# Query copies one unit sooner, and another order of eight small matmuls in odd units

## The chip, the cores and the metric

The kernel runs on one core of a Trainium2 chip. The metric is the device time of one execution in microseconds (us). One execution of the kernel before was also recorded by the hardware profiler, and the profile and the trace below are of that one.

## The reference

Two attention blocks are computed on inputs of 2048 tokens and 448 features, forward and backward, from bfloat16 data. Block A is linear attention with 16 heads. Block B is softmax attention with 16 query heads of 28 features that share one key head and one value head:

```
q = heads(x @ wq);  k = x @ wk;  v = x @ wv
p = softmax(q k^T * 28**-0.5);  o = p v;  out = concat_heads(o) @ wo
```

The outputs are the forward result of both blocks (side by side) and the gradients for all eight inputs, given the gradient of the result. The two changes lie in block B, in the stage that computes the scores, the softmax and their gradients.

## The kernel before

Block A and the projections of block B come first. Then comes the stage of interest, which we call the core. It is one loop over u, written out by hand in the order in which each engine is to take its instructions (a manual schedule: nothing is reordered by a planner). The queries are cut into 64 blocks b of 256 tokens and two heads (b = 8 * qc + pair, where qc counts the eight slices of 256 tokens and pair the eight pairs of heads). Each block is walked in 8 units of 256 keys, so there are 512 units, and u % 8 is the unit's place in its block. A unit u works on several things that are at different stages:

- **Scores.** rows_SD (lines 683 to 705) issues eight small matmuls. Four are score quarters S: head 0 and head 1, each for two groups of 128 keys, of 32 x 128 weights and 256 columns. We write S0a, S0b for head 0 and S1a, S1b for head 1. ScalarE turns them into exponentials: exp0 (line 955) takes both S0 quarters, exp1 (line 997) both S1 quarters. In the trace these are the tiles aacc (scores) and eT (exponentials).
- **Gradients of the probabilities.** The other four matmuls of rows_SD are gradient quarters D0a, D0b, D1a, D1b for the unit w = u - 16. In the trace they are agen<-doT. VectorE multiplies D0 with the exponentials (line 967, into dsT). D1 is first copied by ScalarE (line 971, tile cp) and then multiplied by GpSimd (line 972). A pair of banks holds D, one for each head, so D0 of a unit waits until line 967 of the unit before has read its bank, and D1 until line 971 of the unit before has.
- **Transposes and sums.** VectorE transposes dsT of unit u - 18 (line 1041, into dsx). In odd units dk_m sums the key gradient on TensorE (sixteen matmuls agen<-dsx,qX); in even units o_dq sums the output and the query gradient (sixteen matmuls from eT and dsT).
- **Once per block.** At u % 8 = 1 VectorE copies the block's output sums (line 983); at u % 8 = 2 TensorE transposes them into a spare score bank (line 809) and VectorE copies them out of it (line 817), and GpSimd does three small products (lines 821, 830, 831). The next unit's S0a goes into that same bank. At u % 8 = 4 GpSimd does two more small products (lines 836, 837), and at u % 8 = 6 TensorE transposes their result don (line 845) and VectorE copies it (line 852).
- **Query copies.** dk_m takes its weights from a tile qX, one for each slice of 256 tokens, in which the queries are transposed. It is made one slice ahead, in four groups g. For each group GpSimd makes two copies with gaps into a staging tile qst (line 856, called at line 979), in two units one after the other, and SyncE then issues a DMA transpose from qst to qX (line 860, called at line 1002). There is one tile qst for all groups, so the first copy of a group waits until the transfer of the group before has landed. This runs in the units with u % 64 from 30 to 55, for u below 448: two units out of every eight.
- **Transposes of the exponentials.** At every u % 4 = 3 SyncE issues a DMA transpose of four units' exponentials (line 999, eN<-eT), ahead of line 1002 in the same unit. TensorE reads it at least nine units later. The transposes of lines 860 and 999 go through SyncE's one queue in the order in which they are issued.

In rows_SD, d[0] picks S (0) or D (1) and d[1] the head; a pair's first occurrence in the list is its quarter a, its second is b. S uses two of TensorE's four groups of 32 rows, D the other two, and each head one of them: so S0, S1, D0 and D1 have a group of rows each.

Of the kernel before, what the change touches and what calls it, by code (L numbers as in the profile page):

```python
# [25 lines left out]
def kernel(  # L26
# [624 lines left out]
    with ExitStack() as cs_:  # L651
# [23 lines left out]
        def mmt(out, lhsT, rhs, pos, start, stop):  # L675
            nc.tensor.matmul(out, lhsT=lhsT, rhs=rhs, start=start, stop=stop, tile_position=pos,  # L676
                             skip_group_check=True)

        def blk(b):
            qc, pair = divmod(b, 8)  # L680
            return qc, pair, pair // 2, pair % 2

        def rows_SD(u, sp, dp):
            b, tp = divmod(u, 8)
            w = u - 16
            qc, pair, g, hp = blk(b)
            todo = [(0, 0), (0, 1)] * 2 + [(1, 0), (1, 1)] * 2
            if u % 2 == 0:
                todo = [(0, 0), (0, 1), (1, 0)] * 2 + [(1, 1)] * 2
            seen = {}  # L690
            for d in todo:
                if (dp if d[0] else sp) is None:
                    continue
                k, h = d
                t2 = seen.get(d, 0)
                seen[d] = 1
                t = 2 * tp + t2
                tc_ = slice(t * P, (t + 1) * P)
                oc = slice(t2 * 256, (t2 + 1) * 256)
                r = 64 * (1 - hp if k else hp) + 32 * h  # L700
                if k:
                    mmt(dp[h][:, oc], vT_rep[r:r + 32, tc_], doT[w // 8][r:r + 32, :], (r, 0), True, True)
                else:
                    mmt(sp[h][:, oc], kT_rep[r:r + 32, tc_], qT_B[g][r:r + 32, qc * 256:(qc + 1) * 256],
                        (r, 0), True, True)
# [216 lines left out]
        with tc.manual_schedule():  # L922
# [8 lines left out]
            for u in range(NU + 28):  # L931
# [4 lines left out]
                dp = DB if hasD else None  # L936
                spare = SB[(2 * u + 2) % 3] if hasS else DB[u // 4 % 2] if u > 530 else SB[2]
                rows_SD(u, sp, dp)
                if u % 2 == 0:
                    b, n = divmod(u - 20, 8)  # L940
# [22 lines left out]
                if hasD:  # L963
# [6 lines left out]
                    cp = pc_.tile([P, 512], BF16, name="cp")  # L970
                    nc.scalar.activation(out=cp[:, :], in_=dp[1][:, :], func=ACT.Copy)  # L971
                    nc.gpsimd.tensor_tensor(out=dst[:, 1, :], in0=cp[:, :], in1=ew[:, 1, :], op=ALU.mult)  # L972
                gq, iq = divmod(u % 64 - 30, 8)
                qq = u // 64 + 1
                if 0 <= gq < 4 and u < 448:
                    if gq == 0 and iq == 0:
# [183 lines left out]
```

## Time and profile before

| | us |
|---|---|
| median of 3 runs (lowest to highest) | 1047.6 (1046.28 to 1047.8) |
| the profiled execution | 1045.81 |
| its span, from the first instruction to the end of the last | 1044.1 |

| engine | busy us | share of the span |
|---|---|---|
| TensorE (PE) | 1003.6 | 96% |
| VectorE (DVE) | 887.4 | 85% |
| ScalarE (ACT) | 865.8 | 83% |
| GpSimd (POOL) | 811.9 | 78% |

The core's units run from about 207 us to about 997 us of the span. A row of the timeline gives the start in us, the duration in us, the engine, the line, the operation, the tile it writes and those it reads, how many instructions of that kind are merged into the row, and in brackets the idle time of the engine just before and what ended it. Records of one engine can overlap by a little, since the next instruction starts while the last one drains. SPq is SyncE's queue. The profiler models the ends of matmuls, so for TensorE only the starts are read here.

### The profile page before, as it was taken

How to read it: one execution, taken by the hardware profiler on the slowest of the kernel's cores; microseconds unless marked ns; L12 is line 12 of the kernel's file. 1: busy time of each engine (PE TensorE's matmuls, PEld its weight loads, DVE VectorE, ACT ScalarE, POOL GpSimd, SP SyncE). 2: the span in 40 equal slices, each digit the busy share in tenths (PEclk: the TensorE clock that was granted, in tenths of full speed). 3: DMA queues.
4: the chain of work that ended last, by engine and by line, in shares of the span. 5: the costliest groups of instructions: out<-in, count | busy, mean ns of one | idle time of the engine just before them, and what ended most of it. 6: DMA issues, size and time to landing. Idle time of an engine off the chain costs nothing.

```text
span 1044.1 us, 40103 instructions
## 1 busy us (share of the span) xinstructions
PE 1003.6 (96%) x16236; PEld 485.1 (46%) x16245; DVE 887.4 (85%) x1780; ACT 865.8 (83%) x1743; POOL 811.9 (78%) x1106
## 2 busy tenths in 40 slices
PE   9999999998899999999999999999999999999998
PEld 5555555434444444444444444444444444444444
DVE  7898500669899999999999999999999999999942
ACT  6463132599999999999999999999999999999632
POOL 8601282238898999999999989999998999888860
PEclk9999999999999999999999999999999999999999
DMA  9879999199999999999999999999999999999983
GB/s 266 150 134 195 184 232 213 32 161 205 189 183 198 191 188 195 198 190 189 201 198 197 190 190 203 194 193 198 202 184 201 191 199 192 192 194 197 218 159 90
DMA packets 689059, 195.15 MB, mean 187 GB/s; under 512 B 670409, under 2 KB 686689, under 8 KB 688873
## 3 DMA queue, kind: packets, MB, share of 16 engines
q1 hardware_dynamic: 680392, 179.97, 103.7%
q0 software_dynamic: 4544, 9.46, 3.1%
q10 hardware_dynamic: 3936, 3.16, 1.1%
q8 instruction: 127, 2.08, 0.8%
q14 instruction: 60, 0.48, 0.2%
HBM read 12.60 MB, written 10.84 MB: 22 GB/s over the span
## 4 chain that ended last, share of the span: by engine, by line
PE 37%; DVE 28%; POOL 17%; issue 9%; ACT 8%; DMA 0%; DVEq 0%; POOLq 0%; ACTq 0%
PE agen L81 13%; POOL dsT L972 12%; DVE dsT L967 12%; DVE dsx L1041 10%; PE agen L676 8%; PE aacc L676 7%; PE aacc L81 6%; ACT cp L971 4%; ACT eT L997 2%; DVE doT L852 1%; DVE R L986 1%; POOL qst L856 1%; POOL prod L821 1%; PE aacc L809 1%; DVE Dq L835 1%
## 5 line engine op out<-in xcount | busy, mean ns | idle before, releaser
L972 POOL TENSOR_TENSOR dsT<-cp,eT 128x512 bf16<-128x512 bf16 x512 | 584.1, 1156 | 45.5 <-ACT cp L971 39.8
L1041 DVE STREAM_TRANSPOSE dsx<-dsT 128x512 f32<-128x512 f32 x512 | 357.2, 698 | 8.7 <-POOL dsT L972 5.9
L676 PEld LDWEIGHTS <-R 32*128 32x128 bf16 (+1 forms) x9104 | 245.1, 94 | 246.5 <-issue 195.4
L967 DVE TENSOR_TENSOR dsT<-agen,eT 128x512 bf16<-128x512 f32 x512 | 340.3, 665 | 9.7 <-PE agen L676 4.1
L971 ACT ACTIVATE cp<-agen 128x512 bf16<-128x512 f32 x512 | 326.2, 637 | 12.2 <-PE agen L676 10.3
L955 ACT ACTIVATE eT<-aacc 128x512 bf16<-128x512 f32 x512 | 325.3, 635 | 12.6 <-PE agen L676 6.7
L997 ACT ACTIVATE eT<-aacc 128x512 bf16<-128x512 f32 x512 | 332.4, 649 | 0.0
L676 PE MATMUL agen<-dsx,qX 32*32 32x512 bf16 x4024 | 264.0, 376 | 0.0
L676 PE MATMUL agen<-doT,R 32*128 32x256 bf16 x2048 | 241.6, 269 | 4.1 <-DVE dsT L967 2.6
L676 PE MATMUL aacc<-R,R 32*128 32x256 bf16 (+1 forms) x2240 | 208.3, 267 | 18.9 <-DVE doT L852 7.5
L676 PE MATMUL agen<-dsT,R 128*32 128x256 bf16 x2048 | 155.8, 273 | 0.3 <-POOL dsT L972 0.2
L676 PE MATMUL agen<-eT,R 128*32 128x256 bf16 x2048 | 155.7, 273 | 0.1
L676 PEld LDWEIGHTS <-qX 32*32 32x32 bf16 x4096 | 78.2, 89 | 112.4 <-issue 54.1
L676 PE MATMUL aacc<-eN,don 128*32 128x512 bf16 x1024 | 90.6, 387 | 0.0
L81 PEld LDWEIGHTS <-R 128*128 128x128 bf16 x517 | 40.9, 98 | 41.4 <-issue 11.0
L856 POOL COPY qst<-R 128x512 bf16<-128x512 bf16 x56 | 34.3, 613 | 11.2 <-DMA qX<-qst 5.7
L81 PE MATMUL agen<-R,R 128*128 128x448 bf16 (+1 forms) x174 | 41.1, 360 | 1.7 <-issue 0.6
L676 PEld LDWEIGHTS <-don 128*32 128x32 bf16 x1024 | 20.9, 93 | 40.6 <-issue 40.6
L821 POOL TENSOR_TENSOR prod<-R,oTs 128x128 f32<-128x128 bf16 x64 | 27.5, 430 | 9.0 <-DVE oTs L817 9.0
L586 DVE TENSOR_TENSOR osb<-R 32x512 bf16<-32x512 bf16 x4 | 1.7, 414 | 35.4 <-ACT R L583 35.4
L262 POOL TENSOR_SCALAR wdq<-wdq 128x448 bf16<-128x448 bf16 x16 | 21.1, 1327 | 12.8 <-DVE phiT L243 12.8
L427 POOL COPY pk<-R 128x256 bf16<-128x256 bf16 x4 | 1.6, 400 | 37.7 <-DVE R L389 37.7
(235 smaller groups left out, 1001.2 us busy)
## 6 DMA issues: line engine op xcount, KB each, us to landing
eN<-eT SPq DMA_TRANSPOSE x128
xa<-in_A_x_dram SPq DMA_DIRECT2D x8, 224.0 KB
ga<-in_grad_out_dram SPq DMA_DIRECT2D x4, 448.0 KB
out_dram<-osb ACTq DMA_DIRECT2D x16, 112.0 KB
xa<-in_grad_out_dram POOLq DMA_DIRECT2D x4, 448.0 KB, 8.3
out_dram<-wdq POOLq DMA_DIRECT2D x8, 224.0 KB, 5.1
eT<-in_grad_out_dram SPq DMA_DIRECT2D x4, 448.0 KB
eT<-in_B_x_dram SPq DMA_DIRECT2D x4, 448.0 KB
```

Of the source, the lines that this page charges most:

```text
L81: nc.tensor.matmul(out_ap, lhsT=lhsT, rhs=rhs, start=start, stop=stop, tile_position=(0, 0))
L262: nc.gpsimd.tensor_scalar(out=wq_n[:, st, 0:D], in0=wq_n[:, st, 0:D], scalar1=1.0, scalar2=None, op0=ALU.min)
L676: nc.tensor.matmul(out, lhsT=lhsT, rhs=rhs, start=start, stop=stop, tile_position=pos, skip_group_check=True)
L809: nc.tensor.transpose(onp[:, qb, :, :].rearrange("p h c -> p (h c)"), oTs[0:64, qb * P:(qb + 1) * P], identF[0:64, 0:64], tile_position=(0 ...
L821: nc.gpsimd.tensor_tensor(out=prod[b][:], in0=dnv, in1=os_, op=ALU.mult)
L856: eng.tensor_copy(out=st.rearrange("p (b s) a j -> p b s a j", s=2)[:, :, s, :, :], in_=src.unsqueeze(2).to_broadcast([P, 4, 4, 32]))
L955: nc.scalar.activation(out=eT(u)[:, 0, :], in_=sp[0][:, :], func=ACT.Exp, scale=scale)
L967: nc.vector.tensor_tensor(out=dst[:, 0, :], in0=dp[0][:, :], in1=ew[:, 0, :], op=ALU.mult)
L971: nc.scalar.activation(out=cp[:, :], in_=dp[1][:, :], func=ACT.Copy)
L972: nc.gpsimd.tensor_tensor(out=dst[:, 1, :], in0=cp[:, :], in1=ew[:, 1, :], op=ALU.mult)
L997: nc.scalar.activation(out=eT(u)[:, 1, :], in_=sp[1][:, :], func=ACT.Exp, scale=scale)
L1041: nc.vector.transpose(out=dsx[b][:, tp, :, :, :].rearrange("p h t c -> p (h t c)").bitcast(F32), in_=dsT[y][:, :, :].rearrange("p h c -> p ...
```

## The change

Two lines are edited, and no work is added or removed.

In odd units the eight matmuls of rows_SD are issued in the order S0a S1a S0b D1a S1b D1b D0a D0b; before, it was S0a S1a S0b S1b D0a D1a D0b D1b. Even units keep S0a S1a D0a S0b S1b D0b D1a D1b.

The query copies run in the units with u % 64 = 29 and 30, 37 and 38, 45 and 46, 53 and 54, one unit sooner than before, and the DMA transpose of a group is issued in the second of them. That unit has u % 4 = 2, so the transpose of a group now goes into SyncE's queue one unit ahead of a transpose of exponentials; before, it went in right behind that one. The allocation of the tile qX moves with it.

```
@@ rows_SD
-            todo = [(0, 0), (0, 1)] * 2 + [(1, 0), (1, 1)] * 2
+            todo = [(0, 0), (0, 1), (0, 0), (1, 1), (0, 1), (1, 1), (1, 0), (1, 0)]
             if u % 2 == 0:
                 todo = [(0, 0), (0, 1), (1, 0)] * 2 + [(1, 1)] * 2
...
@@ the loop over u
-                gq, iq = divmod(u % 64 - 30, 8)
+                gq, iq = divmod(u % 64 - 29, 8)
                 qq = u // 64 + 1
                 if 0 <= gq < 4 and u < 448:
                     if gq == 0 and iq == 0:
                         qX[qq] = (pqb_ if qq % 2 else pqa_).tile([P, 4, 2, 512], BF16, name="qX")
                     if iq < 2:
                         qc_copy(nc.gpsimd, qst, qq, gq, iq)
...
                     if 0 <= gq < 4 and iq == 1 and u < 448:
                         qc_T(qst, qq, gq)
```

More of the change, by code (lines that the diff above doesn't have):

```diff
@@ L686, in rows_SD @@
             qc, pair, g, hp = blk(b)
-            todo = [(0, 0), (0, 1)] * 2 + [(1, 0), (1, 1)] * 2
+            todo = [(0, 0), (0, 1), (0, 0), (1, 1), (0, 1), (1, 1), (1, 0), (1, 0)]
             if u % 2 == 0:
@@ L972 @@
                     nc.gpsimd.tensor_tensor(out=dst[:, 1, :], in0=cp[:, :], in1=ew[:, 1, :], op=ALU.mult)
-                gq, iq = divmod(u % 64 - 30, 8)
+                gq, iq = divmod(u % 64 - 29, 8)
                 qq = u // 64 + 1
```

## The prediction

> **What bounds the kernel now.** I read the page first, for who is busy and who waits, then the core in strips of equal work, then single units in the timeline.
>
> ```profile
> L955 ACT ACTIVATE eT<-aacc 128x512 bf16<-128x512 f32 x512 | 325.3, 635 | 12.6 <-PE agen L676 6.7
> ...
> L856 POOL COPY qst<-R 128x512 bf16<-128x512 bf16 x56 | 34.3, 613 | 11.2 <-DMA qX<-qst 5.7
> ```
>
> ScalarE's exp0 (L955) was kept waiting by TensorE for up to 12.6 us in all. It is the first of ScalarE's three instructions in a unit, so a wait there holds up the unit. GpSimd idled 11.2 us ahead of its 56 query copies (L856). The next view shows that the two go together. I cut the core at the starts of exp0 into strips of 32 units, and took those seven in which query copies run (units 32 to 63 of each 64); ScalarE's exp0 alone is counted, so that each strip holds 32 of them.
>
> ```profile
> core 0: us, ACT busy (x), PEclk, DMA share, GB/s
> 252.83:303.36 50.53, 19.78 (x32) 1.00 1.14 186
> ...
> 541.36:588.48 47.12, 20.80 (x32) 1.00 1.18 198
> ...
> 732.64:779.76 47.12, 20.80 (x32) 1.00 1.19 187
> ...
> sum 339.34, ACT 142.32; mean ACT 20.33
> ```
>
> The same work takes 47.12 us in two strips, up to 50.53 in others, and 339.34 in the seven. If all took 47.12, it would be 329.84: so 9.5 us are lost in strips with query copies, though two strips with as many copies lose nothing against the best. What differs is a wait, and the view of the copies' line names it.
>
> ```profile
>   DMA qX<-qst: 5.7, 7
>   DVE dsx L1041: 3.4, 2
>   DVE dsT L967: 2.1, 1
> ```
>
> Ten first copies of a group waited, 5.7 + 3.4 + 2.1 = 11.2 us. Seven are put down to the transfer from qst. Of the other three VectorE is named; a copy needs nothing of VectorE there, so I read the same transfer into them. SyncE's queue shows how the transfers stand, and the timeline of one group how its lateness ends at ScalarE.
>
> ```profile
> 645.81 11.16 SPq L999 DMA_TRANSPOSE eN<-eT  x2
> 657.03 1.30 SPq L860 DMA_TRANSPOSE qX<-qst  x1
> 658.43 11.01 SPq L999 DMA_TRANSPOSE eN<-eT  x2
> 669.54 1.26 SPq L860 DMA_TRANSPOSE qX<-qst  x1
> ```
>
> ```profile
> 656.85 0.71 DVE L1041 STREAM_TRANSPOSE dsx<-dsT 128x512 f32<-128x512 f32 x1 [0.47 <-POOL dsT L972]
> ...
> 657.32 0.23 PE L845 MATMUL aacc<-identB,don 128*32 128x128 bf16 x2 [0.16 <-POOL don L837]
> ...
> 658.51 0.28 PE L676 MATMUL aacc<-R,R 32*128 32x256 bf16 x2 [0.47 <-DVE doT L852]
> ...
> 658.92 0.60 ACT L955 ACTIVATE eT<-aacc 128x512 bf16<-128x512 f32 x1 [0.57 <-PE agen L676]
> ...
> 660.99 0.61 POOL L856 COPY qst<-R 128x512 bf16<-128x512 bf16 x1 [0.41 <-DMA qX<-qst]
> ...
> 674.02 0.61 POOL L856 COPY qst<-R 128x512 bf16<-128x512 bf16 x1 [1.29 <-DVE dsx L1041]
> ```
>
> SyncE works without a pause: two transposes of exponentials (11.16 and 11.01 us), then one for the queries. The query transfer issued at 657.03 releases the copy at 660.99, and that of 669.54 the copy at 674.02: 4.0 and 4.5 us from issue to use. While GpSimd is behind, VectorE waits for its product (0.47), TensorE for the small product don and for VectorE's copy of it (0.16 and 0.47), and ScalarE in the end for scores (0.57 us idle).
>
> In undisturbed units all three of ScalarE, VectorE and TensorE are nearly full: 47.12 / 32 = 1.47 us a unit. One unit with u % 8 = 1, which is odd (the second of the strip that begins at 541.36), shows the chain:
>
> ```profile
> 541.49 1.16 POOL L972 TENSOR_TENSOR dsT<-cp,eT 128x512 bf16<-128x512 bf16 x1
> ...
> 541.84 0.63 ACT L971 ACTIVATE cp<-agen 128x512 bf16<-128x512 f32 x1
> ...
> 542.27 0.70 DVE L1041 STREAM_TRANSPOSE dsx<-dsT 128x512 f32<-128x512 f32 x1
> ...
> 542.41 0.28 PE L676 MATMUL aacc<-R,R 32*128 32x256 bf16 x2
> 542.42 0.28 PE L676 MATMUL agen<-doT,R 32*128 32x256 bf16 x1
> 542.51 0.27 PE L676 MATMUL aacc<-R,R 32*128 32x256 bf16 x1
> 542.53 0.26 PE L676 MATMUL agen<-doT,R 32*128 32x256 bf16 x1
> ...
> 542.54 0.36 PE L676 MATMUL agen<-doT,R 32*128 32x256 bf16 x2
> ...
> 542.82 0.64 ACT L955 ACTIVATE eT<-aacc 128x512 bf16<-128x512 f32 x1
> ...
> 542.89 0.68 DVE L967 TENSOR_TENSOR dsT<-agen,eT 128x512 bf16<-128x512 f32 x1
> ...
> 543.49 0.41 DVE L983 COPY oTs<-agen 64x256 f32<-64x256 f32 x1
> ...
> 543.81 0.28 PE L676 MATMUL aacc<-R,R 32*128 32x256 bf16 x2
> ...
> 543.82 0.69 DVE L1041 STREAM_TRANSPOSE dsx<-dsT 128x512 f32<-128x512 f32 x1
> ...
> 544.26 0.66 ACT L955 ACTIVATE eT<-aacc 128x512 bf16<-128x512 f32 x1
> 544.44 0.64 DVE L967 TENSOR_TENSOR dsT<-agen,eT 128x512 bf16<-128x512 f32 x1
> ...
> 545.02 0.27 DVE L817 COPY oTs<-aacc 128x128 f32<-128x128 f32 x1
> ...
> 545.34 0.28 PE L676 MATMUL aacc<-R,R 32*128 32x256 bf16 x2
> ...
> 545.75 0.65 ACT L955 ACTIVATE eT<-aacc 128x512 bf16<-128x512 f32 x1
> ```
>
> At 542.41 S0a and S1a start, at 542.42 D0a. Then D1a waits until ScalarE's copy of the unit before is done (541.84 + 0.63 = 542.47) and starts at 542.53, D0b at 542.54, D1b 0.1 later. VectorE's product of D0 starts at 542.89, in VectorE's own turn: its six instructions from 542.27 to 545.02 start as fast as each lets the next. The last (L817) frees the bank for the S0a of 545.34, and exp0 follows at 545.75. So whatever makes the product of 542.89 late makes exp0 of two units on late.
>
> **The order of matmuls.** D1a is now ahead of S1b, D1b and both quarters of D0, and all of these are queued behind its wait. S0 keeps its place, so exp0 has its scores as before. S1b now follows D1a (542.53), and exp1 takes it only after exp0 and cp: no cost. D1 cannot be sooner, since its wait ends when it ended; its cover is ScalarE's own turn. D0 is what moves: D0a no longer starts at 542.42, ahead of the wait, but behind it at about 542.54, and D0b, in the same rows, one matmul (0.11) later, at 542.65 in place of 542.54. What this costs needs the time from D0b to VectorE's start where VectorE really waits for it; the unit 40 units later shows that:
>
> ```profile
> 601.74 0.37 PE L676 MATMUL agen<-doT,R 32*128 32x256 bf16 x3
> ...
> 602.06 0.69 DVE L967 TENSOR_TENSOR dsT<-agen,eT 128x512 bf16<-128x512 f32 x1 [0.20 <-PE agen L676]
> ```
>
> D0b at 601.74 (the row's second, right behind D1a), product at 602.06 after 0.20 us idle: 0.32 us. So in the unit above the product could start at 542.65 + 0.32 = 542.97 instead of 542.89: 0.08 later. VectorE runs without a gap from there to L817, S0a waits for L817, and exp0 for S0a; so 0.08 us a block. In a unit like the one 40 later, where VectorE already waits, it is 0.11. In the other odd units VectorE is itself late (at u % 8 = 5 D0a waits for it, and then the order does not matter) or has been shifted by the same 0.08 already. From the 64 blocks I take off two that have no gradients yet and, as an estimate from the code, some twelve in which a wide output projection brings the scores after ScalarE's copy, so that D1a does not wait: 50 x 0.08 = 4.0 us. The bounds are 0, if the trace's idle-free VectorE hides it, and 50 x 0.11 = 5.5. The eight odd units of the drain, without scores, are not on this chain; at 0.11 each they would add 0.9.
>
> That sum lets matmuls pass each other: D0a, fifth in the old order, started at 542.42, ahead of S0b at 542.51, which was issued before it but waited for S0a's rows. If they kept the order of issue, the new list would take one step more (rivals, below). The Trainium skill says just that: "TensorE: Matmul & The Clock Gate", section "Part 3: Packing small matmuls — row/col tiling", has matmuls start and end in program order, with only weight loads pulled ahead. The rows here disagree in the starts, and the measurement decides; the ends are modelled and show nothing.
>
> **The copies.** No copy is saved: 56 at 613 ns before and after. What moves is the transfer: it is issued one unit (1.47 us) sooner and ahead of one transpose of exponentials, half of 11.16 = 5.6 us, instead of behind it. The next group's copy asks 1.47 sooner, too. So the transfer gains about 5.6 us on its reader, if the copy is done by the time SyncE comes to it; even if SyncE has to wait a unit for the copies, 4 us are left. The ten waits have a mean of 1.1 us, and none is above 3.4 (two make up that sum). I count them as gone, and with them the 9.5 us; for a remainder in the first strip, where SyncE is furthest behind, I take off 0.5: gain 9.0. The other bound is 0.
>
> What is late next? On GpSimd each copy is moved past one product (L972), so two products a group end 0.6 us later than before. The one that starts at 541.49 ends at 542.65, and VectorE transposes its result at 543.82: 1.2 us of cover for 0.6. On SyncE one transpose in two goes 1.3 us later (the 1.27 and 1.30 above); its reader comes nine units later or more, over 13 us. If SyncE waits for a copy, only such transposes stand behind it. The tile qX is taken a unit sooner, at u % 64 = 29, where its last reader was at 25. All this I cost at nothing.
>
> **The sum.** -9.0 + 4.0 = -5.0 us. The profiled execution, 1045.81, would be 1040.8. The median of the runs is 1.8 us above it, and I put the change on the median: 1047.6 - 5.0 = 1042.6.
>
> **The rivals.**
>
> *The order costs nothing.* VectorE's product has other slack, or D0a still slips ahead of the wait. Then 1047.6 - 9.5 = 1038.1. For it: 0.08 us is small. Against it: idle-free rows up to L817. Chance 0.13.
>
> *The order takes most of the gain.* If VectorE is pushed by the whole step of 0.11 in every block, or by part of it in two places of a block without catching up in between, that is 64 x 0.11 = 7.0, and 1047.6 - 9.0 + 7.0 = 1045.6. VectorE has little slack anywhere, which speaks for it; in the unit shown 0.03 of the 0.11 is slack, which speaks against. Chance 0.15.
>
> *Matmuls keep the order of issue (slower).* Then in odd units S0a, then S0b D1a S1b, then D1b D0a, then D0b take a step of 0.11 more than before, on TensorE itself. It has almost no room: exp0 started 542.82 - 542.41 = 0.41 after S0a and again 545.75 - 545.34 = 0.41 where TensorE set it, and 544.26 - 543.81 = 0.45 behind an odd unit, so 0.04 is free. It decides from 0.04 on: 0.07 x 4 odd units x 60 blocks = 17 us, and 1047.6 - 9.0 + 17 = 1055.6. This is the page's rule named above. The starts speak against it: chance 0.10.
>
> *The copies fall at a worse place (slower).* At u % 8 = 5 GpSimd is still behind from the three small products and don. If the products of units 5 and 6 then come after VectorE asks for them, each group costs what is over the cover, and the gain is turned into a new wait. It decides when GpSimd is 0.6 us further behind than in the unit above; at 0.3 us of new wait for each of the 28 groups, 8.4 in all, it comes to 1047.6 - 9.0 + 8.4 + 4.0 = 1051.0. The two strips without waits, where GpSimd does the same work, speak against it. Chance 0.09.
>
> *The waits do not go.* The transfer lands late whatever its place. Then 1047.6 + 4.0 = 1051.6; the steady 4.0 to 4.5 us from issue to use speak against it. Chance 0.03.
>
> **How the numbers follow.** The forecast has 0.50, at 1040 to 1044.6. Something within 0.2% (2.1 us, about what a measurement of this kernel can tell from no change) comes mostly from the second rival. Faster by more: 0.50 + 0.13 + half of the second, 0.70. Same: 0.09. Slower: the last three, 0.22 less what stays near nothing, 0.21. The range runs from the first rival, 1038.0, to 1050.5, so that only the in-order case and most of the last two lie above it.
>
> **What would show it.** Right: no idle time before L856 from the transfer; strips of 32 units with copies as long as those without; at u % 8 = 1 D0b about 0.12 us behind D1a, VectorE idle for some 0.08 before L967, and exp0 at u % 8 = 3 that much later; undisturbed strips 47.4 rather than 47.12 us. Wrong: D0 starting ahead of D1a's wait, a step more between the first and the last of the eight matmuls, or VectorE's transposes (L1041) waiting for GpSimd at u % 8 = 0 and 1 of copy groups.

## The result, and the profile after

| | before | after |
|---|---|---|
| median of the runs, us | 1046.95 (7 runs, 1045.61 to 1047.8) | 1043.18 (7 runs, 1042.32 to 1044.75) |
| the profiled execution, us | 1045.81 | 1042.77 |
| its span, us | 1044.1 | 1041.1 |

The changed kernel is faster: the ratio is 0.9968, with a 95% interval of 0.9957 to 0.9980, which is 3.4 us (2.1 to 4.5). The forecast was 5.0 us faster, at 1042.6; the time of 1043.18 lies nearer to it than the gain does, since the kernel before came out at 1046.95 here and not at 1047.6.

The page after, with the two groups that were shown of before (busy time, mean ns of one, idle time ahead of it):

```profile
L955 ACT ACTIVATE eT<-aacc 128x512 bf16<-128x512 f32 x512 | 318.9, 623 | 7.6 <-PE agen L676 3.3
...
L856 POOL COPY qst<-R 128x512 bf16<-128x512 bf16 x56 | 34.2, 611 | 1.3 <-DMA qX<-qst 1.1
```

The idle time ahead of the copies has fallen from 11.2 to 1.3 us, and that ahead of exp0 from 12.6 to 7.6. The view of the copies' line names what is left:

```profile
  DMA qX<-qst: 1.1, 3
```

Three waits, 1.1 us, in place of ten. The same strips as before, of 32 units with query copies each:

```profile
core 0: us, ACT busy (x), PEclk, DMA share, GB/s
252.75:300.27 47.52, 19.73 (x32) 1.00 1.16 187
...
538.03:585.55 47.52, 20.08 (x32) 1.00 1.20 193
...
823.79:871.71 47.92, 20.05 (x32) 1.00 1.21 193
sum 333.21, ACT 139.82; mean ACT 19.97
```

The strips are now nearly alike, and 6.1 us shorter in sum (339.34 before). But the best of them takes 47.52 us where it took 47.12: without any wait the changed kernel is slower, by 0.4 us in 32 units, which is 0.1 a block. The unit that the prediction took apart (u % 8 = 1, the second of the strip that begins at 538.03) shows where that comes from:

```profile
538.51 0.63 ACT L971 ACTIVATE cp<-agen 128x512 bf16<-128x512 f32 x1
...
538.94 0.70 DVE L1041 STREAM_TRANSPOSE dsx<-dsT 128x512 f32<-128x512 f32 x1
...
539.08 0.37 PE L676 MATMUL aacc<-R,R 32*128 32x256 bf16 x3
539.20 0.26 PE L676 MATMUL agen<-doT,R 32*128 32x256 bf16 x1
539.20 0.28 PE L676 MATMUL aacc<-R,R 32*128 32x256 bf16 x1
539.21 0.39 PE L676 MATMUL agen<-doT,R 32*128 32x256 bf16 x3
539.49 0.64 ACT L955 ACTIVATE eT<-aacc 128x512 bf16<-128x512 f32 x1
...
539.65 0.69 DVE L967 TENSOR_TENSOR dsT<-agen,eT 128x512 bf16<-128x512 f32 x1
...
541.79 0.27 DVE L817 COPY oTs<-aacc 128x128 f32<-128x128 f32 x1
...
542.11 0.28 PE L676 MATMUL aacc<-R,R 32*128 32x256 bf16 x2
...
542.52 0.60 ACT L955 ACTIVATE eT<-aacc 128x512 bf16<-128x512 f32 x1
```

ScalarE's copy ends at 538.51 + 0.63 = 539.14, D1a starts at 539.20, and no D0 starts before it; before, D0a went ahead of the wait. VectorE's product starts 0.16 us after exp0 (539.49 to 539.65), where it was 0.07 (542.82 to 542.89). From the product on, all steps are as long as before: 2.14 us to L817 (2.13 before), 0.32 to S0a (0.32), 0.41 to exp0 (0.41). So exp0 of u % 8 = 3 follows that of u % 8 = 1 by 3.03 us, where it was 2.93.

One thing is easily misread: the row of 539.65 has no idle time in brackets. Records of VectorE overlap by up to 0.08 us when nothing is late (the transpose before ends at 539.64 by its record). A delay shorter than that shows only between starts: the product follows the transpose by 0.71 us here, by 0.62 in the unit of before.

What neither the page nor these views say is why a kernel that loses 0.1 us a block, and has 1.1 us of waits at the copies in place of 11.2, gains 3.4 us and not more. For that I read SyncE's queue over the whole core. Before, with the row of one set of exponentials (L997) beside its transpose:

```profile
214.36 10.55 SPq L999 DMA_TRANSPOSE eN<-eT  x2
...
601.25 43.09 SPq L999 DMA_TRANSPOSE eN<-eT  x8
644.44 1.27 SPq L860 DMA_TRANSPOSE qX<-qst  x1
...
960.31 4.84 SPq L999 DMA_TRANSPOSE eN<-eT  x1
966.44 4.93 SPq L999 DMA_TRANSPOSE eN<-eT  x1
...
971.75 0.60 ACT L997 ACTIVATE eT<-aacc 128x512 bf16<-128x512 f32 x1
...
972.38 4.93 SPq L999 DMA_TRANSPOSE eN<-eT  x1
```

After:

```profile
214.27 10.53 SPq L999 DMA_TRANSPOSE eN<-eT  x2
...
638.50 1.25 SPq L860 DMA_TRANSPOSE qX<-qst  x1
639.85 11.49 SPq L999 DMA_TRANSPOSE eN<-eT  x2
...
938.25 38.08 SPq L999 DMA_TRANSPOSE eN<-eT  x7
```

Most rows begin where the one before ends: 601.25 + 43.09 = 644.34, and 644.44 is next. A merged row can hide pauses, though, and the last seven transposes before, taken one by one, have them: between the three shown the queue is free for 1.29 and 1.01 us, and the last starts 0.03 us after the exponentials that it takes are done (971.75 + 0.60 = 972.35). Between these seven it pauses for 5.4 us in all; ahead of them no pause is longer than 0.55 us. After the change no pause is longer than 0.45 us, to the end.

The queue works from 214.36 to 977.32 before (763.0 us) and from 214.27 to 976.33 after (762.1 us), and the core, from the first exp0 to the last, takes 763.2 and 760.2 us. So the queue has next to no room in this stage: before, it just keeps up with the core, and after the change it never catches up. A transpose of exponentials starts a median of 3.0 us after its data are ready before and 6.4 us after, and after the change never less than 1.3 us. The change didn't shorten the queue's work; it let the other engines get further ahead of it, since the last exp0 stands 6.5 us ahead of the queue's end before (970.78) and 8.6 us after (967.70).

### The profile page after: what moved, and what is told of

Read it like the earlier page. It is cut to its first block, busy times and chain, and to the rows that moved or that the text cites. A ratio compares the mean times of both kernels' runs of the same rounds, so it can differ in the third digit from the quotient of the medians.

```text
span 1041.1 us, 40109 instructions
## 1 busy us (share of the span) xinstructions
PE 1003.6 (96%) x16245; PEld 487.0 (47%) x16245; DVE 891.6 (86%) x1780; ACT 868.5 (83%) x1743; POOL 812.2 (78%) x1106
## 4 chain that ended last, share of the span: by engine, by line
PE 40%; DVE 35%; ACT 8%; issue 8%; POOL 6%; DMA 2%; DVEq 0%; SPq 0%; POOLq 0%; ACTq 0%
DVE dsT L967 15%; PE agen L81 13%; DVE dsx L1041 13%; PE agen L676 10%; PE aacc L676 9%; PE aacc L81 5%; POOL dsT L972 4%; ACT cp L971 4%; ACT eT L997 3%; DVE R L986 2%; PE aacc L809 2%; DVE doT L852 2%; DVE oTs L817 1%; DVE Dq L835 1%; DMA eN<-eT 1%
## 5 line engine op out<-in xcount | busy, mean ns | idle before, releaser
L676 PEld LDWEIGHTS <-R 32*128 32x128 bf16 (+1 forms) x9104 | 247.6, 94 | 240.6 <-issue 185.1
L971 ACT ACTIVATE cp<-agen 128x512 bf16<-128x512 f32 x512 | 320.7, 626 | 11.7 <-PE agen L676 10.9
L997 ACT ACTIVATE eT<-aacc 128x512 bf16<-128x512 f32 x512 | 327.1, 639 | 0.0
L955 ACT ACTIVATE eT<-aacc 128x512 bf16<-128x512 f32 x512 | 318.9, 623 | 7.6 <-PE agen L676 3.3
L676 PE MATMUL agen<-doT,R 32*128 32x256 bf16 x2048 | 236.9, 268 | 2.2 <-DVE dsT L967 1.3
L676 PE MATMUL aacc<-R,R 32*128 32x256 bf16 (+1 forms) x2240 | 214.5, 268 | 18.8 <-DVE doT L852 7.8
```

The costliest lines, as they stand in the source:

```text
L955: nc.scalar.activation(out=eT(u)[:, 0, :], in_=sp[0][:, :], func=ACT.Exp, scale=scale)
L997: nc.scalar.activation(out=eT(u)[:, 1, :], in_=sp[1][:, :], func=ACT.Exp, scale=scale)
```

## The experiments

All ratios are to runs of the kernel before that were measured beside the run. "The core" is the time from the first to the last of the 512 starts of exp0 in the profiled execution. My theory after the result: the copies' gain and the order's price are each about as forecast, but both meet a full queue, so they don't add. The rivals: the copies bring less than 9 us in any case; or the order costs more than 4, by matmuls that keep the order of issue.

### The order alone

```
-            todo = [(0, 0), (0, 1)] * 2 + [(1, 0), (1, 1)] * 2
+            todo = [(0, 0), (0, 1), (0, 0), (1, 1), (0, 1), (1, 1), (1, 0), (1, 0)]
```

> The kernel before with only the new order in odd units; the query copies stay. Theory (the new order puts D0 behind D1a's wait, 0.08 us a block through VectorE at u % 8 = 1): 3 to 6 us slower than before, with exp0 at u % 8 = 3 about 0.1 us later in each block and the waits of the copies as before. Rival (the order costs nothing and the copies bring little): within 1 us of before. Rival (matmuls keep the order of issue): 15 us slower or more.

Measured: 1048.03 us (12 runs), ratio 1.0000 (0.9984 to 1.0015). By itself the order costs nothing that can be measured, against 3 to 6 us expected, though its step of 0.1 a block is there: the undisturbed strip takes 47.51. The waits of the copies, expected as before, have become fewer:

```profile
  DMA qX<-qst: 5.5, 6
  DVE dsx L1041: 2.7, 2
```

That is 8.2 us in eight waits, where it was 11.2 in ten. The strips with copies say the same:

```profile
444.52:492.03 47.51, 20.02 (x32) 1.00 1.19 190
...
634.80:684.20 49.40, 19.98 (x32) 1.00 1.17 195
...
sum 337.96, ACT 139.28; mean ACT 19.90
```

Over seven times its own best, 7 x 47.51 = 332.57, the kernel loses 5.4 us here, where before lost 9.5.

### The copies alone

```
-                gq, iq = divmod(u % 64 - 30, 8)
+                gq, iq = divmod(u % 64 - 29, 8)
```

> The kernel before with only the query copies and their transfer one unit sooner. Theory (the transfer's place was the cause of the waits, and the order costs the rest): 8 to 9.5 us faster than before, 1037.5 to 1039, strips of 32 units with copies at 47.1 to 47.3 us. Rival (the copies bring only what the whole change brings): 3 to 4 us faster.

Measured: 1043.59 us (8 runs), ratio 0.9954 (0.9936 to 0.9973), 4.8 us faster and not 9. Without the new order some of the waits are there again:

```profile
  DMA qX<-qst: 7.1, 7
```

The execution that was profiled, 1047.69, is the slowest of its runs, so this row shows the kind of the loss and not its usual size.

### The transfer ahead of the exponentials of its own unit

The copies stay where they were before; only lines 999 and 1002 change places.

```
+                    if 0 <= gq < 4 and iq == 1 and u < 448:
+                        qc_T(qst, qq, gq)
                     if u % 4 == 3:
                         nc.sync.dma_start_transpose(ENs[u // 4 % 6][:, :, :],
...
-                    if 0 <= gq < 4 and iq == 1 and u < 448:
-                        qc_T(qst, qq, gq)
```

> The kernel before, with the copies in their old units, but the transfer issued ahead of the transpose of exponentials of the same unit instead of behind it. Theory (what counts is the place in SyncE's queue, ahead of 5.6 us of another transfer): the waits at the copies go nearly as in the whole change, 7 to 9.5 us faster than before. Rival (the unit sooner on GpSimd is what counts): under 2 us faster, with waits of 5 us or more left at the copies.

Measured: 1043.75 us (12 runs), ratio 0.9965 (0.9950 to 0.9979). The place in the queue, without an earlier copy, is worth as much as the whole change. The view of the waits shows what the queue does instead:

```profile
PE aacc L676 <- DMA eN<-eT: 5.5, 8, 1.3
...
POOL qst L856 <- DMA qX<-qst: 2.8, 4, 0.8
```

The copies wait 2.8 us, and now TensorE waits for the transposed exponentials, eight times, 5.5 us. (This execution, 1046.25, is again the slowest of its runs.) The prediction counted that reader as over 13 us away. The lateness has gone to the other reader of the same queue.

### Odd units in pairs

The new place of the copies, with an order in which every quarter b follows its quarter a at once:

```
-            todo = [(0, 0), (0, 1)] * 2 + [(1, 0), (1, 1)] * 2
+            todo = [(0, 0)] * 2 + [(0, 1)] * 2 + [(1, 0)] * 2 + [(1, 1)] * 2
...
-                gq, iq = divmod(u % 64 - 30, 8)
+                gq, iq = divmod(u % 64 - 29, 8)
```

> Copies one unit sooner, and in odd units the order S0a S0b S1a S1b D0a D0b D1a D1b: every second matmul asks for the rows that the one ahead of it uses, and both quarters of D0 are ahead of D1a's wait. Theory (a matmul whose rows are taken does not hold up those behind it in other rows, and D0 pays only when it is behind D1a's wait): within 1 us of the copies alone, or faster by up to 1. Rival (matmuls keep the order of issue): two steps of 0.11 us more in each odd unit, 25 us slower than the copies alone or more.

Measured: 1043.80 us (10 runs), ratio 0.9960 (0.9943 to 0.9977): the same as the copies alone. TensorE's rows for one odd unit show why (start, duration):

```profile
541.97 0.29 PE L676 MATMUL aacc<-R,R 32*128 32x256 bf16 x2
541.99 0.28 PE L676 MATMUL agen<-doT,R 32*128 32x256 bf16 x1
542.08 0.29 PE L676 MATMUL aacc<-R,R 32*128 32x256 bf16 x2
542.11 0.37 PE L676 MATMUL agen<-doT,R 32*128 32x256 bf16 x3
```

The list is S0a S0b S1a S1b D0a and so on. Two scores start at 541.97 and D0 at 541.99; the other two scores start 0.11 later, with the rows of heads 0 and 1 free again. So S1a and D0a start ahead of S0b, which was issued before them. Kept in the order of issue, this list would take two steps of 0.11 more than the old one, where the prediction's rival counted one and 17 us. It is not slower, and the rival falls. Nor is a price hidden by the queue, as that of the order alone is: the same strip of 32 units takes as long as before the change.

```profile
538.00:585.12 47.12, 20.86 (x32) 1.00 1.18 198
```

### Half the transposes, with the old kernel, with the order, and with the whole change

To see what the queue costs, three kernels relieve it: from unit 24 on, each transpose of exponentials moves two units instead of four. The other two are left out, so the value gradient is summed from old data, and only the time is of use.

```
+                        m = 4 if u < 24 else 2
-                        nc.sync.dma_start_transpose(ENs[u // 4 % 6][:, :, :],
-                                                    ETs[u // 4 % 5][:, :, :, :].rearrange("p a b c -> p (a b c)"))
+                        nc.sync.dma_start_transpose(ENs[u // 4 % 6][:, 0:8 * m, :],
+                                                    ETs[u // 4 % 5][:, 0:m, :, :].rearrange("p a b c -> p (a b c)"))
```

The second adds the line of the order, the third that and the line of the copies.

> The kernel before, but from unit 24 on each transpose of exponentials takes two units instead of four: half of them are left out, so the value gradient is summed from old data. Theory (SyncE's queue of transposes is nearly full and is the second bound, so waits at the copies come from it): the waits at the copies vanish without any move of the copies, all strips run at 1.47 us a unit, and it is 7 to 10 us faster than before. Rival (the place of the copies on GpSimd is the cause): under 2 us faster.

> The same relief (half of the transposes of exponentials left out from unit 24 on), with the new order in odd units. Theory (the order costs 0.1 us a block on VectorE, which the slower pace gave back to the queue in the run of the order alone): 4 to 6 us slower than the same relief with the old order. Rival (the order costs nothing in itself, as its run alone seems to say): within 1.5 us of it.

> The same relief with the whole change, order and copies. Theory (the place of the copies is worth something only while the queue is full): within 1 us of the relief with the new order alone, so 4 to 6 us slower than the relief with neither. Rival (copies one unit sooner are worth 4 us or more by their place on GpSimd): as fast as the relief with neither.

Measured, each against 1047.26 for the kernel before (13 runs):

| queue relieved | us | ratio (95%) | the core, us |
|---|---|---|---|
| old order, old copies | 1037.12 (5 runs) | 0.9900 (0.9885 to 0.9914) | 754.4 |
| new order, old copies | 1042.09 (6 runs) | 0.9946 (0.9933 to 0.9960) | 759.05 |
| new order, new copies | 1041.28 (6 runs) | 0.9944 (0.9929 to 0.9959) | 759.0 |

The first is 10.5 us faster than before, by the ratio. Its queue (the transposes have line 1000 there) now pauses, for 2.7 and 2.6 us in these rows, and its copies never wait; the strips with copies are as long as the others:

```profile
628.23 1.93 SPq L1000 DMA_TRANSPOSE eN<-eT  x1
632.89 1.23 SPq L860 DMA_TRANSPOSE qX<-qst  x1
634.23 7.85 SPq L1000 DMA_TRANSPOSE eN<-eT  x2
644.67 2.04 SPq L860 DMA_TRANSPOSE qX<-qst  x1
```

```profile
536.51:583.63 47.12, 20.80 (x32) 1.00 0.74 117
...
sum 330.57, ACT 143.60; mean ACT 20.51
```

330.57 in place of 339.34 is 8.8 us, and the core is 8.8 us shorter: all that the relief brings to the core lies in the strips with copies, which is the 9 us of the prediction. The second kernel gives the price of the order, 1042.09 - 1037.12 = 5.0 us, of which 4.65 lie in the core:

```profile
538.11:585.63 47.52, 20.08 (x32) 1.00 0.71 116
...
sum 332.84, ACT 139.82; mean ACT 19.97
```

The third shows that the new place of the copies is worth nothing once the queue has room: its ratio and its core are those of the second. Less is moved in these kernels, too (117 GB/s in these strips, 198 before), so a relief of the queue and one of the DMA engines behind it aren't told apart. A transpose of two units takes a median of 2.0 us in the first of them, less than half of the 5.4 us for four; that speaks for a queue that is held in part by the transfers behind it, but it is argued, not shown.

### The groups of copies further apart

If the groups only crowd the queue for half of each 64 units, spreading them should bring the relief without less work. First 11 units apart instead of 8, with the old order:

```
-                gq, iq = divmod(u % 64 - 30, 8)
+                gq, iq = divmod(u % 64 - 29, 11)
```

> The old order; the four groups of copies of a slice start 11 units apart instead of 8, from u % 64 = 29. The queue then has 2.75 transposes of exponentials between two of queries instead of 2. Theory (the queue overflows only while copies run): waits at the copies under 1 us in all, strips of 32 units with copies at 47.1 to 47.6 us, and 7 to 9 us faster than before, 3 or more faster than the copies one unit sooner alone. Rival (the lag of the queue is set by its mean load, or GpSimd is hurt where the copies now fall): no faster than the copies one unit sooner alone.

Measured: 1043.98 us (8 runs), ratio 0.9964 (0.9949 to 0.9979). No copy waits, and the waits have gone elsewhere:

```profile
DVE dsx L1041 <- POOL dsT L972: 3.9, 12, 0.4
...
PE aacc L676 <- DMA eN<-eT: 1.2, 1, 1.2
```

VectorE waits for GpSimd's products, since the copies now fall at other places of a block, and once TensorE waits for the exponentials. Then 16 units apart, so that the load is even over the core:

```
-                gq, iq = divmod(u % 64 - 30, 8)
-                qq = u // 64 + 1
-                if 0 <= gq < 4 and u < 448:
+                gq, iq = divmod((u - 22) % 64, 16)
+                qq = (u - 22) // 64 + 1
+                if 0 <= gq < 4 and 22 <= u < 470:
...
-                    if 0 <= gq < 4 and iq == 1 and u < 448:
+                    if 0 <= gq < 4 and iq == 1 and 22 <= u < 470:
```

> The old order; the groups of query copies start 16 units apart, in the old place of a block (u % 8 = 6 and 7), from u % 64 = 22 on, the last group in the slice after. The queue then has four transposes of exponentials between two of queries. Theory (the queue overflows only because the transfers of the queries are crowded into half of the units): no waits at the copies, no wait for transposed exponentials, 8 to 9.5 us faster than before (1037.5 to 1039.5), so 4 or more faster than the whole change. Rival (the queue's mean load is too high whatever the spacing): 4 to 5 us faster than before, as the copies alone.

Measured: 1045.03 us (12 runs), ratio 0.9974 (0.9962 to 0.9986). It isn't the crowding: with even load the queue is as full, and TensorE waits for it.

```profile
611.26 1.26 SPq L860 DMA_TRANSPOSE qX<-qst  x1
612.63 21.66 SPq L999 DMA_TRANSPOSE eN<-eT  x4
634.39 1.25 SPq L860 DMA_TRANSPOSE qX<-qst  x1
635.73 22.57 SPq L999 DMA_TRANSPOSE eN<-eT  x4
```

```profile
PE aacc L676 <- DMA eN<-eT: 2.9, 4, 0.9
```

From 611.26 to 634.39 the queue spends 23.1 us on 16 units, and from there to the next query transfer 24.0 (658.35, not shown). Undisturbed units need 16 x 1.4725 = 23.6 us, by the 47.12 for 32. The queue's work is as long as ScalarE's, with nothing to spare.

The same with pairs in all units, as a second test of the order of issue:

```
-            todo = [(0, 0), (0, 1)] * 2 + [(1, 0), (1, 1)] * 2
-            if u % 2 == 0:
-                todo = [(0, 0), (0, 1), (1, 0)] * 2 + [(1, 1)] * 2
+            todo = [(0, 0)] * 2 + [(0, 1)] * 2 + [(1, 0)] * 2 + [(1, 1)] * 2
```

> The same spacing, and in all units the order S0a S0b S1a S1b D0a D0b D1a D1b. Even units so have S0b ahead of D0a, which waits for VectorE. Theory (matmuls in other rows are not held up, and a score behind VectorE's wait makes exp0 late): 0 to 4 us faster than the spacing alone. Rival (matmuls keep the order of issue): 40 us slower or more. Rival (D1 last in even units holds up cp): a few us slower.

Measured: 1045.12 us (12 runs), ratio 0.9973 (0.9956 to 0.9990), against 0.9974 without the pairs. The order of issue has no price here either, and the pairs bring no gain.

### The copies two units sooner

The old order, as it is free of the 0.1 a block, and one unit more for the copies:

```
-                gq, iq = divmod(u % 64 - 30, 8)
+                gq, iq = divmod(u % 64 - 28, 8)
```

> The old order, copies two units sooner than before (u % 64 = 28 and 29): the transfer stands in the same place in SyncE's queue as when they are one unit sooner, but the copies stand right behind GpSimd's small products at u % 8 = 4. Theory (the place in the queue counts): within 2 us of the copies one unit sooner, 2 to 6 us faster than before. Rival (GpSimd is hurt there): VectorE's transposes wait for GpSimd by 10 us or more, and it is slower than before.

Measured: 1042.24 us (4 runs), ratio 0.9941 (0.9920 to 0.9963). It has the lowest ratio of the versions that do all the work, but its interval reaches into that of the change (0.9957 to 0.9980) and into most of that of the copies alone, so it isn't shown to beat them. Its waits are small in each place, and not gone:

```profile
DVE dsx L1041 <- POOL dsT L972: 3.7, 10, 1.4
...
POOL qst L856 <- DMA qX<-qst: 2.5, 3, 1.5
```

## Why the prediction was right in direction and 1.6 us too high in gain

The profiled executions can be summed. The relieved kernels have the core's length without any wait from the queue: 754.4 us with the old order, 759.05 with the new. What a kernel has above that it loses to the queue:

| | the core, us | without the queue | lost to the queue |
|---|---|---|---|
| before | 763.2 | 754.4 | 8.8 |
| the order alone | 764.2 | 759.05 | 5.15 |
| after | 760.2 | 759.05 | 1.15 |

So the change took 8.8 - 1.15 = 7.65 us from the waits and gave 4.65 to the order: -3.0 us, as the profiled executions differ. The prediction had -9.0 and +4.0. The medians, which come from different sets of runs, point the same way: less the medians of the relieved kernels, 10.1 us are lost before, 5.9 with the order alone and 1.9 after, and 6.5 with the copies alone.

That the sum came within 1.6 us of the gain is in part luck. Taken alone, the copies gave 4.8 us in place of 9.0 and the order cost nothing in place of 4.0, and the two errors offset each other.

**The copies' term.** "I count them as gone" holds for nearly all of the waits (11.2 to 1.1 us, those put down to VectorE included), and the 9.5 us worked out from the strips was the right size of the loss (8.8 in the core of the relieved kernel). What failed is the step that made it the change's own gain. With the old order the same move gave 4.8 us, and with the queue relieved none. I had quoted that SyncE works without a pause, in four rows, and read it as a transfer that comes late; I did not follow the queue over the core. It has next to no room over the core, and so what is taken from one of its readers can come back at another. "All this I cost at nothing" was the sentence: the transposes of exponentials that go later did not have 13 us of cover. In the changed kernel they start up to 9.8 us after their data are ready, and each takes 5.4 us. TensorE waits for them 0.4 us there, and 5.5 us in the kernel with the transfer ahead of them.

**The order's term.** The mechanism was found as told: D0 behind D1a's wait, VectorE's product at u % 8 = 1 late, then L817, S0a, exp0. It was priced at 0.08 us a block and is 0.10, 4.65 us in the core against 4.0. But it was added to the gain as if both were on one path. Alone, beside the full queue, it costs nothing that can be measured (1.0000), and the copies' waits fall from 11.2 to 8.2 us: slower units give the queue time. Beside the moved copies it costs 4.8 - 3.4 = 1.4 us, by ratios whose intervals overlap, where it costs 5.0 with the queue relieved. That the difference is given back through the queue there too is argued: only 1.15 us are lost in the changed kernel, while waits are left in the copies alone. No run shows a gain from the new order.

**The rivals.** *The order costs nothing* and *takes most of the gain*: neither; 4.65 us in the core with the queue relieved. *Matmuls keep the order of issue*: refuted by the two kernels in pairs. The changed kernel agrees: the last row of its eight matmuls begins at 539.21, 0.01 us behind D1a, and that start can't be D1b's, which waits for D1a's rows (0.11 us); it is D0a's, which was issued behind D1b. *A worse place on GpSimd*: not in the changed kernel, where VectorE waits 0.3 us for products; one unit earlier still, it is 3.7. *The waits do not go*: they went, in the changed kernel.

**What would show it.** As listed: no more than 1.1 us of the transfer's waits, strips alike, D0 behind D1a, undisturbed strips of 47.5 (forecast 47.4). VectorE's idle time ahead of the product isn't in the records, since it is shorter than their overlap; the starts show it.

## What to carry to other kernels

Before pricing a wait on a transfer, follow the queue that serves it over the whole stage: where its rows join without a pause (taken one by one, since merged rows hide pauses) and its work is as long as the stage, taking a wait away can move the lateness to the next reader, and a small loss elsewhere may cost nothing. The worths of two edits that meet the same full resource can't be added; run each alone, and both with the resource relieved. Look for delays in the distance between starts, since a delay shorter than the overlap of two records has no idle time.

## What the runs showed that I had not expected

- A queue of transposes can be a bound without any engine's share of busy time telling it. Transposes of four units of exponentials take 5.4 us each (43.09 us for eight), and 16 units' worth with one query transfer takes 23.1 to 24.0 us beside 23.6 of ScalarE's turn.
- A matmul whose rows are busy is passed by later ones on other rows: in pairs, S0a, S1a and D0a started within 0.02 us (541.97 to 541.99), though the list had S0b and S1b between them. The Trainium skill, "TensorE: Matmul & The Clock Gate", section "Part 3: Packing small matmuls — row/col tiling", has matmuls start in program order; the starts here and the two kernels in pairs disagree.
- Executions of a kernel with the full queue lie several us apart: the kernel before went from 1044.38 to 1052.08 (29 runs). With the queue relieved the old order stayed within 1036.65 to 1037.49 (5 runs). That the queue makes the spread is argued, not shown.
